# Softmax scaling on VectorE, products held behind a subtraction, and a rearranged start, in a fused softmax-convolution and tanh MLP

## The chip, the cores and the metric

The kernel runs on one core of a Trainium2 chip. A time is device microseconds of one execution. The kernel before takes 772.08 us (median of 3 runs, 771.82 to 773.02, so within 0.16% of each other). The span of a profile is some 2 us shorter than the time of the run it belongs to (769.8 against 771.89 us for the kernel before).

## The reference

```python
# x: (8, 4096, 192)   weight_gen: (8, 4096, 8 heads, 7)   w_in: (192, 2048)   w_out: (2048, 192)
w = softmax(weight_gen, axis=-1)
x_pad = six rows of zeros in front of each sequence of x
a[b, s, h, g] = sum over k < 7 of w[b, s, h, k] * x_pad[b, s + k, h, g]      # h: head, g: 24 channels
h   = a.reshape(32768, 192) @ w_in
out = (h - tanh(h)) @ w_out
```

## The kernel before

The 32,768 tokens go in 32 superblocks of 1024. For superblock n, ScalarE takes exp of the weights; VectorE sums over k and takes the reciprocal; GpSimd scales the exponentials by it and makes the seven products (tap k of x times its weight), six of them in pairs; a DMA of GpSimd's queue adds the three odd products onto the even ones (the **accumulating DMA**). TensorE adds up and transposes the products by multiplying them with an identity (**conv**, tile pc), ScalarE copies the result out of PSUM (convT), TensorE makes 16 tiles of the hidden layer (**gemm1**, "f tiles", tile ph), ScalarE takes tanh, VectorE subtracts, and TensorE makes the **second product** (gemm2) of the superblock before, between the f tiles. The order of every engine's instructions is fixed by hand.

```python
    def softmax_norm(n):                                   # VectorE
        e_t = e_of.pop(n)
        nc.vector.reduce_sum(out=zsum[:], in_=..., axis=AX.X)
        zr = wgpool.tile([P, J * H], FP32, name="zr")      # in SBUF
        nc.vector.reciprocal(zr[:], zsum[:])
        zr_of[n] = (e_t, zr)
    ...
    def products(n, on_vector=(), hooks={}):
        ...
        scale(nc.gpsimd, wsm[:], e_t, zr)                  # GpSimd
        ...                                                # seven products, accumulating DMA
    ...
    def conv(n, chunks): ...       # matmuls into one bank pc, then ONE copy to convT
    ...
    for n in range(NTOT):
        if n + 3 < NTOT:
            load(n + 3)
        if n + 2 < NTOT:
            products(n + 2)        # as soon as GpSimd gets there
        for p in range(J):
            gemm1(n, 2 * p)
            gemm1(n, 2 * p + 1)
            if p == 5 and n + 3 < NTOT:
                softmax_exp(n + 3)
            if n >= 1:
                gemm2((n - 1) * J + p)
            if n + 1 < NTOT:
                if p == (6 if n > 0 else 7):
                    conv(n + 1, (0, 1))
                    conv(n + 1, (2,))
            if p == 6 and n + 3 < NTOT:
                softmax_norm(n + 3)
```

gemm1 and conv share three PSUM buffers (tag "ph"), so an f tile may start only when the subtraction of the tile three places back has read its buffer (in the trace one such subtraction ends at 298.68 us and gemm1 begins at 298.74).

The softmax here doesn't subtract the row's maximum and nothing guards it: scores larger than these inputs give would overflow.

## Time and profile before

| | before |
|---|---|
| time | 772.08 us |
| TensorE busy / GpSimd busy, of a 769.8 us span | 735.1 / 695.0 us |
| superblock 1 begins (first matmul of gemm1 after conv(1)) | 46.92 us |
| conv(3), conv(31) begin | 93.37, 728.13 us |
| steady round, conv to conv | 22.63 us |

Read it so: from conv(3) on, all rounds but one take 22.63 us, with TensorE busy for 22.61 of them; the one longer round holds the 1.16 us stop that the prediction mentions. On this reading a gain must come from the first 93 us, and a loss can come from anywhere. The page and chain rows are in the prediction.

### The profile page before, as it was taken

To read this page: it belongs to the slowest core of one execution; us is meant where nothing else is said; L and a number is where in the kernel's file an instruction comes from. 1 tells how busy PE (TensorE), PEld (TensorE's weight loads), DVE (VectorE), ACT (ScalarE), POOL (GpSimd) and SP (SyncE) were. 2 spreads that over 40 slices of the span, in tenths; PEclk is the share of its full clock that TensorE was granted. 3 is DMA by queue.
4 is the path that set the end of the run, shared out by engine and by line. 5 is a ranking of instruction groups with operands and counts; after the bars stand their busy time and mean duration, and the time that the engine had idled before them with its cause. 6 is when DMAs were issued, how large, how long until landed. Compare 5 with 4: busy or idle time off the path is not lost.

```text
span 769.8 us, 32365 instructions
## 1 busy us (share of the span) xinstructions
PE 735.1 (95%) x14784; PEld 581.3 (76%) x14784; DVE 653.3 (85%) x594; ACT 640.8 (83%) x865; POOL 695.0 (90%) x291
## 2 busy tenths in 40 slices
PE   1688999999999999999999999999999999999997
PEld 1357777877787877877788778787787777787777
DVE  5876988888898888888888889888888988888883
ACT  1677888888888888888888888888888888888883
POOL 5999999999999999999999999999999999999100
PEclk9899999999999999999999999999999999999999
DMA  8813776555677555577655557765556775542412
GB/s 214 183 75 86 182 182 144 125 144 148 169 181 173 133 130 147 151 178 181 168 119 139 145 159 181 181 132 144 138 149 168 181 181 120 127 139 66 98 43 83
DMA packets 25848, 111.37 MB, mean 145 GB/s; under 512 B 4801, under 2 KB 9457, under 8 KB 21625
## 3 DMA queue, kind: packets, MB, share of 16 engines
q1 hardware_dynamic: 14688, 76.95, 29.9%
q0 software_dynamic: 10816, 31.99, 25.9%
q8 instruction: 115, 1.88, 1.0%
q10 hardware_dynamic: 208, 0.39, 0.2%
q14 instruction: 21, 0.16, 0.1%
HBM read 54.49 MB, written 25.17 MB: 103 GB/s over the span
## 4 chain that ended last, share of the span: by engine, by line
PE 93%; DMA 2%; DVE 2%; issue 1%; POOL 1%; ACT 0%; SPq 0%; POOLq 0%; DVEq 0%; ACTq 0%
PE ph L233 43%; PE po L264 43%; PE pc L210 6%; DVE gt L244 2%; PE po L305 1%; DMA x_t<-in_x_dram 1%; DMA w_in<-in_moe_w_in_dram 1%; DMA wg_t<-in_weight_gen_dram 1%; POOL even L167 0%; ACT th L242 0%; DVE zsum L128 0%; DVE zr L132 0%; POOL w_in L340 0%; SPq L99 0%; SPq L348 0%
## 5 line engine op out<-in xcount | busy, mean ns | idle before, releaser
L244 DVE TENSOR_TENSOR gt<-ph,th 128x1024 bf16<-128x1024 f32 x512 | 602.6, 1219 | 91.6 <-ACT th L242 91.4
L242 ACT ACTIVATE th<-ph 128x1024 f32<-128x1024 f32 x512 | 497.1, 1022 | 63.6 <-PE ph L233 63.2
L233 PE MATMUL ph<-convT,w_in 64*128 64x512 bf16 x3072 | 381.3, 378 | 7.7 <-DVE gt L244 6.8
L264 PEld LDWEIGHTS <-gt 64*128 64x128 bf16 x7936 | 344.4, 94 | 52.5 <-ACT th L242 1.7
L264 PE MATMUL po<-w_out,gt 64*128 64x192 bf16 x7936 | 373.8, 243 | 1.7 <-ACT th L242 1.3
L167 POOL TENSOR_TENSOR even<-x_t,wsm 128x1536 bf16<-128x1536 f32 x94 | 272.8, 2903 | 3.9 <-DMA x_t<-in_x_dram 1.5
L167 POOL TENSOR_TENSOR odd<-x_t,wsm 128x1536 bf16<-128x1536 f32 x92 | 267.0, 2903 | 0.0
L233 PEld LDWEIGHTS <-w_in 64*128 64x128 bf16 x3072 | 179.6, 94 | 109.5 <-issue 13.4
L167 POOL TENSOR_TENSOR last<-x_t,wsm 128x1536 bf16<-128x1536 f32 x31 | 103.4, 3335 | 0.0
L289 ACT ACTIVATE out_sb<-po 128x192 f32<-128x192 f32 x248 | 81.9, 330 | 9.1 <-PE po L264 3.2
L220 ACT ACTIVATE convT<-pc 128x1024 bf16<-128x1024 f32 x64 | 48.7, 808 | 33.4 <-PE pc L210 33.4
L210 PE MATMUL pc<-ident,even 64*128 64x64 bf16 x2304 | 47.8, 191 | 18.4 <-POOL even L167 16.8
L210 PEld LDWEIGHTS <-even 64*128 64x128 bf16 x2304 | 42.2, 96 | 19.2 <-POOL even L167 17.0
L136 POOL TENSOR_TENSOR wsm<-e_t,zr 128x448 f32<-128x448 f32 x32 | 44.4, 1387 | 6.0 <-DVE zr L132 6.0
L176 POOL DMA_DIRECT2D even<-odd x29 | 34.9, 1205 | 9.0 <-POOL odd L167 9.0
L118 ACT ACTIVATE e_t<-wg_t 128x448 f32<-128x448 f32 x32 | 18.5, 578 | 10.9 <-DMA wg_t<-in_weight_gen_dram 10.9
L128 DVE TENSOR_REDUCE zsum<-e_t 128x64 f32<-128x448 f32 x32 | 19.5, 609 | 4.8 <-ACT e_t L118 4.8
L210 PE MATMUL pc<-ident,last 64*128 64x64 bf16 x768 | 22.9, 191 | 0.0
L132 DVE RECIPROCAL zr<-zsum 128x64 f32<-128x64 f32 x32 | 17.7, 553 | 3.2
L210 PE MATMUL pc<-ident,odd 64*128 64x64 bf16 x448 | 15.3, 195 | 3.1 <-issue 3.1
L210 PEld LDWEIGHTS <-last 64*128 64x128 bf16 x768 | 16.8, 96 | 0.0
L210 PEld LDWEIGHTS <-odd 64*128 64x128 bf16 x448 | 11.0, 99 | 3.3 <-issue 3.3
(18 smaller groups left out, 48.0 us busy)
## 6 DMA issues: line engine op xcount, KB each, us to landing
x_t<-in_x_dram SPq DMA_DIRECT2D x24, 1344.0 KB
even<-odd POOLq DMA_DIRECT2D x29, 1024.0 KB, 8.8
out_dram<-out_sb SPq DMA_DIRECT2D x31, 768.0 KB
x_t<-in_x_dram SPq DMA_DIRECT2D x8, 1176.0 KB
wg_t<-in_weight_gen_dram SPq DMA_DIRECT2D x32, 224.0 KB
x_t<-in_x_dram SPq DMA_DIRECT2D x8, 157.5 KB
w_in<-in_moe_w_in_dram POOLq DMA_DIRECT2D x6, 128.0 KB, 7.1
w_out<-in_moe_w_out_dram POOLq DMA_DIRECT2D x1, 768.0 KB, 8.0
```

The source lines that it names most:

```text
L118: nc.scalar.activation(out=e_t[:].rearrange("p j h k -> p (j h k)"), in_=wg_t[:].rearrange("p j h k -> p (j h k)"), func=ACT.Exp,)
L128: nc.vector.reduce_sum(out=zsum[:], in_=e_t[:].rearrange("p j h k -> p (j h) k"), axis=AX.X)
L136: eng.tensor_mul(wsm.rearrange("p j h k -> p (j h) k"), e_t[:].rearrange("p j h k -> p (j h) k"), zr[:].rearrange("p (n o) -> p n o", o=1) ...
L167: eng.tensor_mul(dst[k].rearrange("p c j h g -> p j h c g"), x_t[:, k : k + J, :].rearrange("p j (h c g) -> p j h c g", h=H, c=NC), w[:, : ...
L176: nc.gpsimd.dma_start(out=even[:].rearrange("p i c j h g -> p (i c j h g)")[:, 0:ACC], in_=odd[:].rearrange("p i c j h g -> p (i c j h g)" ...
L210: nc.tensor.matmul(pc[:, r, col : col + R], lhsT=prods[c][gi][r * R : (r + 1) * R, c, 2 * j : 2 * j + 2].rearrange("p j h g -> p (j h g)") ...
L220: nc.scalar.activation(out=convT[:, c0 : c0 + nch, :].rearrange("p c (j r t) -> p r (c j) t", r=2, t=R), in_=pc[:, :, 0 : nch * JH * R].re ...
L233: nc.tensor.matmul(ph[:, r, :], lhsT=w_in[r * R : (r + 1) * R, c, f * P : (f + 1) * P], rhs=convT[r * R : (r + 1) * R, c, :], start=(c == ...
L242: last_act[0] = nc.scalar.activation(out=th[:], in_=ph_f, func=ACT.Tanh)
L244: nc.vector.tensor_sub(gt[:], ph_f, th[:])
L264: mm = nc.tensor.matmul(po[:, 0:D], lhsT=g_of[n][f][r * R : (r + 1) * R, col : col + P], rhs=w_out[r * R : (r + 1) * R, f, :], start=(r == ...
L289: last_act[0] = nc.scalar.activation(out=out_sb[:, j, :], in_=po[:, 0:D], func=ACT.Copy)
```

## The change

Its intent: take the softmax scaling off GpSimd (all but that of superblock 2); let GpSimd begin the products of a superblock at a fixed place in the round; and shorten the start. Cut to its core:

```diff
+    obank = [psum_o.tile([P, 512], FP32, name=f"obank{i}", tag=f"obank{i}") for i in range(2)]
...
+    def softmax_norm(n, bank, in_psum=False):
+        e_t, zsum = softmax_sum(n)
+        zr = bank[:, 512 - J * H : 512]          # 1/sum into a PSUM bank: conv's own
+        nc.vector.reciprocal(zr, zsum[:])
...
+        wsm = wgpool.tile([P, J, H, K], FP32, name="wsm")
+        last_wsm[0] = scale(nc.vector, wsm[:], e_t, zr)
...
-        scale(nc.gpsimd, wsm[:], e_t, zr)
...
+            if k == 0 and behind is not None:
+                order(mul, behind, "pace")       # first product waits for a subtraction
...
     for n in range(NTOT):
-        if n + 2 < NTOT:
-            products(n + 2)
         for p in range(J):
             gemm1(n, 2 * p)
             gemm1(n, 2 * p + 1)
...
+            if p == 0 and 1 <= n < NTOT - 2:
+                products(n + 2, behind=last_sub[0] if n > 1 else None)
             if n + 1 < NTOT:
                 if p == (6 if n > 0 else 7):
                     conv(n + 1, (0, 1))
-                    conv(n + 1, (2,))
+                if p == (6 if n > 1 else 7):
+                    bank = conv(n + 1, (2,))
...
-                softmax_norm(n + 3)
+                softmax_norm(n + 3, bank if n > 0 else obank[0])
```

At the start (not shown): the loads of weights and x are split and reordered, the second half of w_in is issued behind GpSimd's third product instead of its first, VectorE makes four instead of five of the first products, and conv(0) works on both of its parts at once.

More of the change, by code (lines that the diff above doesn't have):

```diff
@@ L59 @@
     psum_h = ctx.enter_context(tc.tile_pool(name="psum_h", bufs=3, space=bass.MemoryType.PSUM))
-    psum_o = ctx.enter_context(tc.tile_pool(name="psum_o", bufs=2, space=bass.MemoryType.PSUM))
+    psum_o = ctx.enter_context(tc.tile_pool(name="psum_o", bufs=1, space=bass.MemoryType.PSUM))
     ident = const.tile([P, P], BF16, name="ident")
     make_identity(nc, ident[:])
+    obank = [psum_o.tile([P, 512], FP32, name=f"obank{i}", tag=f"obank{i}") for i in range(2)]
     zero = const.tile([1, D], FP32, name="zero")
@@ L69 @@
     e_of = {}
-    zr_of = {}
+    wsm_of = {}
     prods_of = {}
@@ L74, with order, load_wg @@
     last_act = {}
-    def load(n):
+    g1_act = {}
+    last_sub = {}
+    last_wsm = {}
+    def order(inst, other, reason):
+        tc.add_manual_dep(
+            inst.ins,
+            other.ins.name,
+            mybir.DependencyInfo(mybir.DependencyClass.Sync, mybir.DependencyReason.DATA),
+            reason=reason,
+        )
+    def load_wg(n):
         b, s = divmod(n, NSB)
@@ L83, in load, with load_x @@
         )
+        wg_of[n] = wg_t
+    def load_x(n):
+        b, s = divmod(n, NSB)
+        s0 = s * TOK
         x_t = xpool.tile([P, HALO + J, D], FP32, name="x_t")
@@ L111, in load @@
             rows(0, P)
-        wg_of[n] = wg_t
         x_of[n] = x_t
@@ L123, in softmax_exp, with softmax_sum @@
         e_of[n] = e_t
-    def softmax_norm(n):
+    def softmax_sum(n):
         e_t = e_of.pop(n)
@@ L130, in softmax_norm, with softmax_norm_gpsimd, products @@
         )
+        return e_t, zsum
+    def softmax_norm(n, bank, in_psum=False):
+        e_t, zsum = softmax_sum(n)
+        zr = bank[:, 512 - J * H : 512]
+        nc.vector.reciprocal(zr, zsum[:])
+        wsm_v = None
+        if in_psum:
+            wsm_v = obank[n % 2][:, 0 : J * H * K].rearrange("p (j h k) -> p j h k", j=J, h=H)
+            scale(nc.vector, wsm_v, e_t, zr)
+        wsm = wgpool.tile([P, J, H, K], FP32, name="wsm")
+        last_wsm[0] = scale(nc.vector, wsm[:], e_t, zr)
+        wsm_of[n] = (wsm, wsm_v)
+    def softmax_norm_gpsimd(n):
+        e_t, zsum = softmax_sum(n)
         zr = wgpool.tile([P, J * H], FP32, name="zr")
         nc.vector.reciprocal(zr[:], zsum[:])
-        zr_of[n] = (e_t, zr)
+        wsm = wgpool.tile([P, J, H, K], FP32, name="wsm")
+        scale(nc.gpsimd, wsm[:], e_t, zr[:])
+        wsm_of[n] = (wsm, None)
     def scale(eng, wsm, e_t, zr):
-        eng.tensor_mul(
+        return eng.tensor_mul(
             wsm.rearrange("p j h k -> p (j h) k"),
             e_t[:].rearrange("p j h k -> p (j h) k"),
-            zr[:].rearrange("p (n o) -> p n o", o=1).to_broadcast([P, J * H, K]),
+            zr.rearrange("p (n o) -> p n o", o=1).to_broadcast([P, J * H, K]),
         )
-    def products(n, on_vector=(), hooks={}):
+    def products(n, on_vector=(), sums=None, hooks={}, behind=None):
         x_t = x_of.pop(n)
-        e_t, zr = zr_of.pop(n)
-        wsm_v = None
-        if on_vector:
-            pw = psum_o.tile([P, 512], FP32, name="pw", tag="po")
-            wsm_v = pw[:, 0 : J * H * K].rearrange("p (j h k) -> p j h k", j=J, h=H)
-            scale(nc.vector, wsm_v, e_t, zr)
-        wsm = wgpool.tile([P, J, H, K], FP32, name="wsm")
-        scale(nc.gpsimd, wsm[:], e_t, zr)
+        wsm, wsm_v = wsm_of.pop(n)
         in_pairs = n not in PLAIN
@@ L166, in products @@
             eng, w = (nc.vector, wsm_v) if k in on_vector else (nc.gpsimd, wsm[:])
-            eng.tensor_mul(
+            mul = eng.tensor_mul(
                 dst[k].rearrange("p c j h g -> p j h c g"),
@@ L189, in products, with conv @@
         else:
-            prods_of[n] = [[dst[k] for k in sorted(range(K), key=lambda k: k in on_vector)]] * NC
-    def conv(n, chunks):
+            prods_of[n] = [[dst[k] for k in (sums or range(K))]] * NC
+    def conv(n, *parts):
         prods = prods_of[n]
@@ L197, in conv @@
         convT = conv_of[n]
-        nch = len(chunks)
-        pc = psum_h.tile([P, 2, HT], FP32, name="pc", tag="ph")
-        steps = [
-            (gi, ci, c)
-            for gi in range(max(len(prods[c]) for c in chunks))
-            for ci, c in enumerate(chunks)
-            if gi < len(prods[c])
-        ]
-        for si, (gi, ci, c) in enumerate(steps):
-            for j in range(JH):
-                col = (ci * JH + j) * R
-                for r in range(2):
-                    nc.tensor.matmul(
-                        pc[:, r, col : col + R],
-                        lhsT=prods[c][gi][r * R : (r + 1) * R, c, 2 * j : 2 * j + 2].rearrange(
-                            "p j h g -> p (j h g)"
-                        ),
-                        rhs=ident[r * R : (r + 1) * R, r * R : (r + 1) * R],
-                        start=(si == 0 and j == 0),
-                        stop=(si == len(steps) - 1 and j == JH - 1),
-                    )
@@ L219, in conv @@
-        c0 = chunks[0]
-        nc.scalar.activation(
-            out=convT[:, c0 : c0 + nch, :].rearrange("p c (j r t) -> p r (c j) t", r=2, t=R),
-            in_=pc[:, :, 0 : nch * JH * R].rearrange("p r (cj t) -> p r cj t", t=R),
-            func=ACT.Copy,
-        )
-        if c0 + nch == NC:
+        pcs = [psum_h.tile([P, 2, HT], FP32, name="pc", tag="ph") for _ in parts]
+        for gi in range(max(len(g) for g in prods)):
+            for chunks, pc in zip(parts, pcs):
+                some = [c for c in chunks if gi < len(prods[c])]
+                last = gi == max(len(prods[c]) for c in chunks) - 1
+                for c in some:
+                    for j in range(JH):
+                        col = ((c - chunks[0]) * JH + j) * R
+                        for r in range(2):
+                            nc.tensor.matmul(
+                                pc[:, r, col : col + R],
+                                lhsT=prods[c][gi][
+                                    r * R : (r + 1) * R, c, 2 * j : 2 * j + 2
+                                ].rearrange("p j h g -> p (j h g)"),
+                                rhs=ident[r * R : (r + 1) * R, r * R : (r + 1) * R],
+                                start=(gi == 0 and c == chunks[0] and j == 0),
+                                stop=(last and c == some[-1] and j == JH - 1),
+                            )
@@ L226, in conv @@
+        for chunks, pc in zip(parts, pcs):
+            c0, nch = chunks[0], len(chunks)
+            nc.scalar.activation(
+                out=convT[:, c0 : c0 + nch, :].rearrange("p c (j r t) -> p r (c j) t", r=2, t=R),
+                in_=pc[:, :, 0 : nch * JH * R].rearrange("p r (cj t) -> p r cj t", t=R),
+                func=ACT.Copy,
+            )
+        if parts[-1][-1] == NC - 1:
             prods_of.pop(n)
+        return pcs[-1][:, 0]
     def gemm1(n, f):
@@ L241, in gemm1 @@
         ph_f = ph[:].rearrange("p r t -> p (r t)")
+        g1_act[0] = last_act.get(0)
         last_act[0] = nc.scalar.activation(out=th[:], in_=ph_f, func=ACT.Tanh)
         gt = gpool.tile([P, TOK], BF16, name=f"gt{f}", tag=f"gt{f}")
-        nc.vector.tensor_sub(gt[:], ph_f, th[:])
+        last_sub[0] = nc.vector.tensor_sub(gt[:], ph_f, th[:])
         g_of.setdefault(n, []).append(gt)
@@ L258, in gemm2 @@
             if r == 0:
-                half[blk] = psum_o.tile([P, 512], FP32, name="po")
+                half[blk] = obank[blk % 2]
             ops.append((r, n, j, half[blk]))
@@ L271, in gemm2 @@
                 if r == 1 and f == 0 and i in (1, LAST):
-                    tc.add_manual_dep(
-                        mm.ins,
-                        last_act[0].ins.name,
-                        mybir.DependencyInfo(
-                            mybir.DependencyClass.Sync, mybir.DependencyReason.DATA
-                        ),
-                        reason="order of the row tiles in a bank",
-                    )
+                    order(mm, g1_act[0] if i == 1 else last_act[0], "row tiles in one bank")
         if i > 0:
@@ L332, in load_w_out, with load_w_in, copy_w_in, rest_of_w_in @@
         nc.gpsimd.dma_start(out=w_out[:], in_=moe_w_out.rearrange("(c p) e -> p c e", c=NFT))
-    HF = F // 2
-    def load_w_in(q):
+    FA = 8 * P
+    def load_w_in(f0, f1):
         for c in range(NC):
-            src = moe_w_in[c * GC : c * GC + 1, q * HF : (q + 1) * HF]
-            nc.gpsimd.dma_start(
-                out=w_in[0:R, c, q * HF : (q + 1) * HF],
+            src = moe_w_in[c * GC : c * GC + 1, f0:f1]
+            dma = nc.gpsimd.dma_start(
+                out=w_in[0:R, c, f0:f1],
                 in_=bass.AP(
-                    tensor=src.tensor, offset=src.offset, ap=[[G * F, H], [F, GC], [1, HF]]
+                    tensor=src.tensor, offset=src.offset, ap=[[G * F, H], [F, GC], [1, f1 - f0]]
                 ),
             )
-    def copy_w_in(q, eng):
-        eng.dma_start(
-            out=w_in[R:P, :, q * HF : (q + 1) * HF], in_=w_in[0:R, :, q * HF : (q + 1) * HF]
-        )
-    load(0)
+            if f0 == 0:
+                order(dma, last_wsm[0], "order of the loads")
+    def copy_w_in(f0, f1, eng):
+        eng.dma_start(out=w_in[R:P, :, f0:f1], in_=w_in[0:R, :, f0:f1])
+    def rest_of_w_in():
+        load_w_in(FA, F)
+    load_wg(0)
+    load_x(0)
     softmax_exp(0)
-    softmax_norm(0)
-    load(1)
+    softmax_norm(0, obank[0], in_psum=True)
+    load_wg(1)
+    load_x(1)
+    load_w_in(0, FA)
     products(
         0,
-        on_vector=(1, 3, 4, 5, 6),
-        hooks={-1: lambda: load_w_in(0), 0: lambda: load_w_in(1)},
+        on_vector=(3, 4, 5, 6),
+        sums=(3, 0, 4, 5, 1, 6, 2),
+        hooks={2: rest_of_w_in},
     )
     softmax_exp(1)
-    softmax_norm(1)
-    copy_w_in(0, nc.scalar)
-    copy_w_in(1, nc.sync)
+    softmax_norm(1, obank[1], in_psum=True)
+    load_wg(2)
+    copy_w_in(0, FA, nc.scalar)
+    copy_w_in(FA, F, nc.sync)
     products(1, on_vector=(0, 1), hooks={4: load_w_out})
-    conv(0, (0, 1))
-    conv(0, (2,))
-    load(2)
-    softmax_exp(2)
-    softmax_norm(2)
+    conv(0, (0, 1), (2,))
+    load_x(2)
     for n in range(NTOT):
         if n + 3 < NTOT:
-            load(n + 3)
-        if n + 2 < NTOT:
-            products(n + 2)
+            load_wg(n + 3)
+            load_x(n + 3)
         for p in range(J):
@@ L378 @@
             gemm1(n, 2 * p + 1)
+            if n == 0 and p == 1:
+                softmax_exp(2)
             if p == 5 and n + 3 < NTOT:
@@ L385 @@
                     conv(n + 1, (0, 1))
-                    conv(n + 1, (2,))
-            if p == 6 and n + 3 < NTOT:
-                softmax_norm(n + 3)
+                if p == (6 if n > 1 else 7):
+                    bank = conv(n + 1, (2,))
+            if n == 0 and p == 2:
+                softmax_norm_gpsimd(2)
+                products(2)
+            if p == (7 if n == 1 else 6) and n + 3 < NTOT:
+                softmax_norm(n + 3, bank if n > 0 else obank[0])
     gemm2(LAST)
```

## The prediction

Its sum came to +0.7 us, 772.8 in all. The passages marked as cut, here and in three of the expectations, are statements on the hardware that did not come from this case's traces, or that rest on such. That the stops of conv(2) are late fetches was my reading at that time, and that splitting conv(2) would shrink them to about half (gain 1.5 of the measured 2.78 us) a guess.

> **What bounds the kernel now.** I read the page's busy shares first, then the chain of waits that ended last, then that chain over one superblock, then the order of time on VectorE and ScalarE at the one place where they come close to TensorE. From the page:
>
> ```profile
> PE 735.1 (95%) x14784; PEld 581.3 (76%) x14784; DVE 653.3 (85%) x594; ACT 640.8 (83%) x865; POOL 695.0 (90%) x291
> PE 93%; DMA 2%; DVE 2%; issue 1%; POOL 1%; ACT 0%; SPq 0%; POOLq 0%; DVEq 0%; ACTq 0%
> ```
>
> From the chain in order of time, one superblock (start us, length us, what):
>
> ```profile
> 297.21 1.52 PE pc L210 x104
> 298.72 0.02 issue
> 298.74 1.47 PE ph L233 x12
> 300.21 1.32 PE po L264 x32
> 301.53 1.30 PE ph L233 x12
> ```
>
> TensorE is 93% of the chain. From 93.54 us on, a superblock takes 22.63 us in the windows view, with TensorE busy 22.61 of it at a granted clock of 1.00. GpSimd looks almost as full (22.25 of 22.63), but no wait of TensorE on a product stands in that part of the chain: conv starts when the stream reaches it. The parts that are not TensorE's lie in the first 75 us; these rows of the chain show them:
>
> ```profile
> 19.98 4.79 DMA wg_t<-in_weight_gen_dram
> ...
> 26.20 0.55 DVE zr L132
> 26.75 1.09 DVE gt L244
> ...
> 51.42 1.03 ACT th L242
> 52.44 0.05 issue
> 52.49 1.49 PE po L264 x31
> ...
> 67.20 0.82 issue
> 68.02 2.04 PE pc L210 x128
> 70.07 1.96 issue
> 72.03 0.59 PE pc L210 x29
> ```
>
> The reader is to see four delays: the third block of weights (wg_t) arrives late and holds VectorE's first subtraction to 26.67; superblock 0 then runs at VectorE's pitch until TensorE begins superblock 1 at 46.92; the second product's first matmul waits for a tanh (52.49); conv(2) stops twice with nothing to wait for (0.82 + 1.96).
>
> [...] Here six pairs of row tiles take 1.29 to 1.30 us, 0.216 each[...]. [...] The trace's GpSimd scaling takes 0.97 us at 36.48 and 57.55 but 1.33 at 5.20 beside VectorE's own two-input scaling[...]. [...] The new code puts 1/sum into conv's own bank, so it must wait for the copy of that bank; no run here shows it yet. [...] Between the two stops of conv(2) lie exactly 128 matmuls with their 128 weight loads, so I read both stops as late fetches; splitting conv(2) over two places should soften them.
>
> **The change, part by part.**
>
> *GpSimd's scaling goes.* 29 instructions of about 1.42 us leave GpSimd in the steady part (row L136, 1387 ns mean over 32). GpSimd's round falls from 22.64 us (scalings start at 283.57 and 306.20) to about 21.2. Worth on the path: 0, since TensorE never waited for it there.
>
> *Pacing.* Products of a superblock now wait for an early subtraction; in the compiled order it is the second (f tile 1) of superblock n, not a later one. It ends at 305.6 on the old clock. Six products at a pitch of 2.86 us end at 322.8; the accumulating DMA lands 8.8 us (its row) after its issue near 323.1, so at 332; conv needs it at 342.5. Slack 10 us, cost 0. Early on GpSimd lags: products(2) should end near 57, products(3) near 77.5 with its DMA at 83, against conv(3) near 85. Tight, but no wait.
>
> *Start, gains.* At 9.85 both engines have x. VectorE has four products instead of five: it ends near 16.6, then sum 0.61, reciprocal 0.55, two scalings of 0.63 to 19.05, two products of 1.75 to 22.4. GpSimd's third product ends at 9.89 + 3 x 2.86 = 18.5; the last 24 conv matmuls and two copies (1.02, 0.59) put the first gemm1 at 20.3 and its tanh's end at 22.3. So the first subtraction starts at about 22.4 instead of 26.67: 4.2 us. Given back: the sum and reciprocal of block 2 move inside the subtractions (1.25), and block 3's scaling adds 0.65. 14 subtractions took 16.8 us before (26.67 to 43.47); 22.4 + 16.8 + 1.25 + 1.95 + 2.3 for the last two gives 44.6, against 46.9: gain 2.3 to 3, I take **2.5**. It needs the second half of w_in, issued only after 18.5, in both halves of SBUF before f tile 8 at about 29.5: old issues took 7 us to land and the copy about 4, so it is due at 28 to 29.5.
> The second product's wait moves one tanh earlier: **0.9** (52.44 to 51.52). The two fetch stops, 2.78, should shrink to about half: **1.5**. The split makes gemm1 of superblock 2 wait for the copy of the third chunk: give back **0.3**.
>
> *Steady part, loss.* The order of time of VectorE, then of ScalarE, over one conv (start, length):
>
> ```profile
> 298.61 0.61 DVE L128 TENSOR_REDUCE zsum<-e_t 128x64 f32<-128x448 f32 x1
> 299.32 0.55 DVE L132 RECIPROCAL zr<-zsum 128x64 f32<-128x64 f32 x1
> 300.66 2.35 DVE L244 TENSOR_TENSOR gt<-ph,th 128x1024 bf16<-128x1024 f32 x2 [0.79 <-ACT th L242]
> ```
>
> ```profile
> 298.18 1.51 ACT L220 ACTIVATE convT<-pc 128x1024 bf16<-128x1024 f32 x2 [0.60 <-PE pc L210]
> 299.60 1.94 ACT L242 ACTIVATE th<-ph 128x1024 f32<-128x1024 f32 x2
> ```
>
> VectorE has 0.79 us to spare before the subtraction of f tile 14, and the added scaling (0.63) would just fit. But the reciprocal must now wait for the second conv copy, which ends at 299.69, instead of starting at 299.32. Then: reciprocal 299.72 to 300.27; scaling, after a gap of 0.10 like that between sum and reciprocal here, 300.38 to 301.01; subtraction 14 starts at 300.93 (consecutive VectorE instructions overlap by about 0.08) instead of 300.66 and ends at 302.14. Its buffer is the one that gemm1's f tile 1 of the next superblock writes: three buffers, 16 + 2 tiles a superblock, so the place repeats each time. That tile starts at 301.35 + 0.65 = 302.00 today. TensorE follows the end of a subtraction by about 0.055 (the subtraction before this conv ends at 298.68, a row at 296.33 of length 2.35, and gemm1 begins at 298.74), so it would start at 302.20: **0.2 us lost** in each of 27 superblocks (2 to 28), 5.3 us. Everything after it has slack again, and the round becomes about 22.83 us.
>
> Sum: -2.5 - 0.9 - 1.5 + 0.3 + 5.3 = +0.7 us.
>
> **The rivals.** (a) *The steady wait isn't there.* Subtraction 14 need only end 0.14 us sooner than I work out for no wait at all; a shorter gap between reciprocal and scaling (0.03 as between other instructions) gives half of it. For: such tuned code was probably laid so as to fit. Against: the wait for the copy is in the compiled program. Then only the start counts: about 767. (b) *GpSimd was the hidden bound*, its round of 22.64 being TensorE's: then its freed 1.4 us a round would bring up to 40 us. Against: when TensorE stopped for 1.16 us at 343.94, the next conv still found its products ready, and gemm1 and the second product alone fill the round at full clock. I give it almost nothing. (c) *A transfer at the start comes too late*, the second half of w_in above all, or the accumulating DMA for conv(3): 1 to 4 us of the gain is lost, and the time is 774 to 777. (d) *VectorE becomes the bound*: 19.92 + 0.63 of 22.63 leaves room; only the local wait above is real.
>
> **Range and chances.** The sum gives 772.8. The loss has more room to shrink than to grow (it sits on margins of 0.1 us), so I predict 771. Rival (a) with a better start gives 765; (c) on top of the sum, or a wait of 0.35 us, gives 777. To be 2% faster the kernel would have to lose 15.4 us, more than all delays of the start that this change touches (4.2 + 0.9 + 2.8); to be 2% slower the round would have to grow by 0.75 us with a gain of 5 at the start. Chances: faster 0.03, same 0.94, slower 0.03.
>
> **What would show it.** Right: a round of about 22.8 between convs, with a wait of TensorE on the subtraction before f tile 1 of each superblock; GpSimd near 21 us a round with idle time that ends at a subtraction; superblock 1 beginning near 44.6; no wait of VectorE on wg_t. Wrong in size: a round still 22.63 (then the time is near 767), or over 23. Wrong in kind: TensorE waiting on products or on the accumulating DMA at conv, VectorE's scaling taking 1 us or more, GpSimd's products longer than 2.90, or a wait on w_in at f tile 8.

## The result, and the profile after

The changed kernel takes **772.24 us** (median of 4 runs, 772.03 to 773.02); the kernel before took 772.51 in the same rounds. The ratio is 0.9999, 95% interval 0.9982 to 1.0016. The result is the same time, out of two large opposite terms:

| | before | after |
|---|---|---|
| superblock 1 begins | 46.92 | 44.30 |
| conv(3) begins | 93.37 | 88.33 |
| steady round | 22.63 | 22.82 |
| conv(31) begins | 728.13 | 728.02 |
| span of the profile | 769.8 | 770.0 |

The lead of 5.0 us at conv(3) is down to 0.1 us at conv(31). From the changed kernel's page, busy times and the chain:

```profile
PE 740.4 (96%) x14784; PEld 578.0 (75%) x14784; DVE 668.6 (87%) x624; ACT 640.9 (83%) x865; POOL 668.3 (87%) x261
PE 93%; DVE 3%; POOL 1%; DMA 1%; ACT 1%; issue 1%; SPq 0%; POOLq 0%; DVEq 0%
```

GpSimd (POOL) lost 27 us of work and VectorE (DVE) gained 15, yet the shares of the chain are nearly those of before: busy time moved, the path did not. The start, in the chain of waits (start us, length us, what):

```profile
41.97 2.28 DVE gt L277 x2
44.25 0.04 issue
44.30 1.58 PE ph L265 x12
...
47.87 1.03 ACT th L275
48.91 0.05 issue
48.95 1.49 PE obank L297 x31
...
67.03 0.94 issue
...
69.72 0.61 ACT convT L251
```

Superblock 1 begins 2.62 us sooner. The second product's wait (48.95) lies 4.65 us behind that, instead of 5.57: another 0.92. Near conv(2) one stop with no cause is left (67.03, 0.94), and the split of conv(2) has made a new wait on a copy (69.72). One conv of the steady part, first the chain, then VectorE's order of time (the bracket gives the idle time ahead of an instruction and what ended it):

```profile
299.00 0.65 PE ph L265 x6
299.65 0.02 issue
299.67 0.82 PE ph L265 x6
```

```profile
296.08 0.61 DVE L145 TENSOR_REDUCE zsum<-e_t 128x64 f32<-128x448 f32 x1
297.19 0.56 DVE L154 RECIPROCAL pc<-zsum 128x64 f32<-128x64 f32 x1 [0.51 <-ACT convT L251]
297.86 0.62 DVE L172 TENSOR_TENSOR wsm<-e_t,pc 128x448 f32<-128x448 f32 x1
298.40 4.70 DVE L277 TENSOR_TENSOR gt<-ph,th 128x1024 bf16<-128x1024 f32 x4
```

Before, two f tiles stood here in one piece of 12 matmuls and 1.30 us; now they are two pieces of six, 1.49 us together: the first matmul of the second piece comes 0.39 us behind the one ahead of it, where the other pairs (two row tiles) come 0.20 behind theirs. VectorE's rows show the reason: the reciprocal stands idle for 0.51 us until ScalarE's copy of conv's bank is done, then reciprocal, scaling and subtraction follow one another. GpSimd's waits hold one new row, the pacing (us in total, times, longest):

```profile
POOL even L195 <- DVE gt L277: 28.2, 25, 1.4
```

### The profile page after: what moved, and what is told of

Read it like the earlier page. It is cut to its first block, busy times and chain, and to the rows that moved or that the text cites. A ratio compares the mean times of both kernels' runs of the same rounds, so it can differ in the third digit from the quotient of the medians.

```text
span 770.0 us, 32309 instructions
## 1 busy us (share of the span) xinstructions
PE 740.4 (96%) x14784; PEld 578.0 (75%) x14784; DVE 668.6 (87%) x624; ACT 640.9 (83%) x865; POOL 668.3 (87%) x261
## 4 chain that ended last, share of the span: by engine, by line
PE 93%; DVE 3%; POOL 1%; DMA 1%; ACT 1%; issue 1%; SPq 0%; POOLq 0%; DVEq 0%
PE ph L265 43%; PE obank L297 43%; PE pc L240 6%; DVE gt L277 2%; PE po L331 1%; DMA x_t<-in_x_dram 1%; POOL even L195 1%; ACT convT L251 0%; ACT th L275 0%; POOL odd L195 0%; DVE wsm L172 0%; DVE zsum L145 0%; SPq L117 0%; DVE pc L154 0%; DVE obank L154 0%
## 5 line engine op out<-in xcount | busy, mean ns | idle before, releaser
L265 PE MATMUL ph<-convT,w_in 64*128 64x512 bf16 x3072 | 385.5, 377 | 7.5 <-DVE gt L277 5.3
L297 PE MATMUL obank<-w_out,gt 64*128 64x192 bf16 x7936 | 373.9, 243 | 1.8 <-issue 0.9
L195 POOL TENSOR_TENSOR even<-x_t,wsm 128x1536 bf16<-128x1536 f32 x94 | 276.8, 2945 | 29.3 <-DVE gt L277 28.2
L195 POOL TENSOR_TENSOR odd<-x_t,wsm 128x1536 bf16<-128x1536 f32 x93 | 273.8, 2945 | 0.0
L265 PEld LDWEIGHTS <-w_in 64*128 64x128 bf16 x3072 | 175.8, 94 | 117.2 <-issue 20.4
L315 ACT ACTIVATE out_sb<-obank 128x192 f32<-128x192 f32 x248 | 82.2, 331 | 14.1 <-PE obank L297 8.7
L154 DVE RECIPROCAL pc<-zsum 128x64 f32<-128x64 f32 x28 | 15.7, 561 | 14.8 <-ACT convT L251 14.8
L172 DVE TENSOR_TENSOR wsm<-e_t,pc 128x448 f32<-128x448 f32 x28 | 17.4, 622 | 2.9
```

Of the source, the lines that this page charges most:

```text
L172: return eng.tensor_mul(wsm.rearrange("p j h k -> p (j h) k"), e_t[:].rearrange("p j h k -> p (j h) k"), zr.rearrange("p (n o) -> p n o", ...
L195: mul = eng.tensor_mul(dst[k].rearrange("p c j h g -> p j h c g"), x_t[:, k : k + J, :].rearrange("p j (h c g) -> p j h c g", h=H, c=NC), ...
L265: nc.tensor.matmul(ph[:, r, :], lhsT=w_in[r * R : (r + 1) * R, c, f * P : (f + 1) * P], rhs=convT[r * R : (r + 1) * R, c, :], start=(c == ...
L297: mm = nc.tensor.matmul(po[:, 0:D], lhsT=g_of[n][f][r * R : (r + 1) * R, col : col + P], rhs=w_out[r * R : (r + 1) * R, f, :], start=(r == ...
L315: last_act[0] = nc.scalar.activation(out=out_sb[:, j, :], in_=po[:, 0:D], func=ACT.Copy)
```

## The experiments

Two things were to be settled. First: is the 0.19 us a round really the wait for the copy, worked out in the prediction? Second: the prediction said of the pacing that it costs nothing and of GpSimd's relief that it is worth nothing, so pacing should be of no account. All runs gave correct results.

| run | time, median | before, same rounds | ratio, 95% interval |
|---|---|---|---|
| scaling back on GpSimd | 770.84 | 771.36 | 0.9994 [0.9982, 1.0005] |
| no pacing | 779.65 | 771.36 | 1.0119 [1.0091, 1.0148] |
| 1/sum in SBUF | 771.21 | 771.36 | 0.9998 [0.9986, 1.0011] |
| before + VectorE scaling | 786.25 | 771.36 | 1.0190 [1.0150, 1.0230] |
| before + VectorE scaling + pacing | 774.01 | 772.05 | 1.0029 [1.0016, 1.0042] |
| f tile 1 later | 767.80 | 772.05 | 0.9944 [0.9931, 0.9956] |
| f tiles 1, 14, 15 later | 764.30 | 772.05 | 0.9904 [0.9890, 0.9918] |
| 1/sum in the bank, then in SBUF | 768.41 | 772.05 | 0.9956 [0.9942, 0.9969] |
| pacing behind f tile 5 | 788.14 | 771.11 | 1.0221 [1.0207, 1.0235] |
| pacing behind f tile 7 | 809.62 | 771.11 | 1.0500 [1.0486, 1.0515] |
| useless work ahead of the reciprocal | 772.13 | 771.11 | 1.0015 [1.0003, 1.0028] |
| useless work behind the scaling | 778.54 | 770.89 | 1.0099 [1.0082, 1.0116] |

### The steady loss

**Scaling back on GpSimd** (pacing and start as changed):

```diff
-                softmax_norm(n + 3, bank if n > 0 else obank[0])
+                softmax_norm_gpsimd(n + 3)
```

> The changed kernel with the steady scaling back on GpSimd (1/sum in SBUF), its start, order and pacing kept. Theory (start gains about 5.2 us, the VectorE chain conv copy, reciprocal, scaling, subtraction 14 gives 0.19 us back in each of 27 rounds): round from conv to conv back to 22.63 us, no wait of TensorE on the subtraction before f tile 1, time 767.1 (766.4 to 768). Rival A (the start's gain is not kept, and the scaling costs nothing): time stays at 772.2. Rival B (the later, paced begin of the products costs the time): stays at 772.2 with the round at 22.82, or gets worse since GpSimd's round is 22.6 again.

Measured: 770.84 us. The undisturbed rounds are back at 22.63 and the gap before f tile 1 is gone, so the scaling's place on VectorE did cause it. But the time is a miss by nearly 4 us: seven stops of TensorE that wait for nothing the profile shows, from 68 to 256 us, took the rest (5.8 us together, where the changed kernel has three with 1.8). They led to the second question, below.

**Useless work on VectorE, ahead of the reciprocal and behind the scaling**: a reduction of 0.32 us, in superblocks 4 to 31.

```diff
         e_t, zsum = softmax_sum(n)
+        if n > 3: nc.vector.reduce_sum(out=zd[:, 0:24], ...)     # first run: here
         zr = bank[:, 512 - J * H : 512]
         nc.vector.reciprocal(zr, zsum[:])
         ...
         last_wsm[0] = scale(nc.vector, wsm[:], e_t, zr)
+        if n > 3: nc.vector.reduce_sum(out=zd[:, 0:24], ...)     # second run: here
```

> The changed kernel with a useless reduction of 24 x 7 elements (about 0.32 us on VectorE) between the sum and the reciprocal, in superblocks 4 to 31. Theory (the reciprocal waits for conv's copy, which ends about 0.4 us behind the sum, so VectorE has idle time just there): costs 0, 772.2 and a round of 22.82, though VectorE gets 28 x 0.32 = 9 us more work. Rival (VectorE is short of time round conv, whatever it does): the round grows by 0.3 us to 23.1 and the time to 780.

> The changed kernel with the same useless reduction (about 0.32 us on VectorE), now behind the scaling instead of ahead of the reciprocal. Theory (from the end of conv's copy on, VectorE's reciprocal, scaling and subtraction 14 set when gemm1 of f tile 1 may start, with no slack left): each of 27 superblocks loses another 0.32 us, round 23.14, time 772.2 + 8.6 = 780.8, range 778.5 to 783. Rival (the wait before f tile 1 is set by something else, or there is slack): 772 to 774, as with the reduction ahead of the reciprocal.

Measured: 772.13 us with the round still 22.82, and 778.54 us with a round of 23.06. The same 9 us of VectorE work costs nothing in one place and 6.3 us (778.54 less the changed kernel's 772.24) two instructions later. (The two stood on different chips; by the ratios the first costs up to about 1 us and the second 7.7, so I go by the rounds, which repeat to 0.01.) The chain of the second run shows the whole loop in order:

```profile
298.93 0.60 ACT convT L258
...
299.55 0.57 DVE pc L154
...
300.21 0.62 DVE wsm L179
300.84 0.24 DVE zd L164
301.07 1.14 DVE gt L284
302.22 0.04 issue
302.26 0.82 PE ph L272 x6
```

Copy, reciprocal, scaling, extra work, subtraction 14, f tile 1. The extra instruction shows as 0.24 and not as its 0.32, since consecutive VectorE instructions overlap by 0.08; 27 x 0.24 = 6.5 us is what was measured. The expectation had used the instruction's length, not its step on the chain.

**1/sum in SBUF**, so that the scaling need not wait for the copy; both of its inputs are then in SBUF:

```diff
-                softmax_norm(n + 3, bank if n > 0 else obank[0])
+                softmax_norm(n + 3, None)          # None: zr is a tile in SBUF
```

> The changed kernel with 1/sum in SBUF, scaling still on VectorE: no wait for conv's copy, but two SBUF inputs while GpSimd runs products of 2.90 us. Theory 1 [...]: VectorE's scaling starts only when the running product ends, up to 2.9 us late, mean near 1.4, so TensorE loses about 1 us or more a round: 795 to 815. Theory 2 [...]: reciprocal at the end of the sum, 0.4 us sooner, subtraction 14 starts when its tanh ends, round 22.63 and time near 767.

Measured: 771.21 us, a steady round of 22.63, and three early scalings that took 1.67, 3.02 and 2.52 us. Behind the first, superblock 1 begins 1.8 us later than in the changed kernel (46.09); behind the other two TensorE stands for 2.1 and 1.4 us. VectorE's and GpSimd's orders of time around the worst of them:

```profile
72.59 3.02 DVE L175 TENSOR_TENSOR wsm<-e_t,zr 128x448 f32<-128x448 f32 x1
```

```profile
72.23 2.90 POOL L198 TENSOR_TENSOR odd<-x_t,wsm 128x1536 bf16<-128x1536 f32 x1
```

GpSimd's product ends at 75.13 and the scaling, which takes 0.62 us with 1/sum in the bank, at 75.61, 0.48 behind it. That the product held it is my reading of these times. In the steady part the end of a product (300.45) and the issue of the accumulating DMA (300.75) come just there, the scaling takes about 0.85 us (300.08 to 300.93), and it costs nothing: the round is 22.63. **1/sum in the bank for superblocks 3 to 6, then in SBUF** joins the two:

```diff
+                softmax_norm(n + 3, obank[0] if n == 0 else bank if n < 4 else None)
```

> The changed kernel with 1/sum in the bank only while GpSimd still lags (superblocks 3 to 6), then in SBUF, where the scaling need not wait for conv's copy. Theory (with pacing the scaling falls between two products of GpSimd[...]; in the run with 1/sum in SBUF from the start it cost up to 2.5 us three times early on): round 22.63 from superblock 5 on and time 772.2 - 24 x 0.195 = 767.5, range 766.5 to 769. Rival ([...] later scalings are held too): 770 to 773.

Measured: 768.41 us. The first SBUF scaling still took 1.40 us, the later ones take from 0.62 to about 0.86; from conv(6) on every round is 22.63.

**f tile 1 later**: gemm1 of f tile 1 goes into the second product that follows it, so that TensorE has other work until subtraction 14 is done; **f tiles 1, 14 and 15 later** does the same for the two behind conv.

```diff
+            if n > 1 and p == 0:
+                gemm1(n, 0)
+                inside[3] = lambda n=n: gemm1(n, 1)           # second run: inside[6], and
+            elif 1 < n < NTOT - 1 and p == J - 1:             # these three lines
+                inside[2] = lambda n=n: (gemm1(n, 2*J - 2), gemm1(n, 2*J - 1))
             else: ...
-                gemm2((n - 1) * J + p)
+                gemm2((n - 1) * J + p, inside)                # calls inside[f] behind step f
```

> The changed kernel with gemm1 of f tile 1 moved into the second product that follows it (behind its f = 3) for superblocks 2 to 31, so that TensorE has other work until subtraction 14 has ended. Theory (the steady loss is that one wait and nothing else): the round goes from 22.82 back to 22.63 and the time to 772.2 - 27 x 0.195 = 767.0, range 766 to 769. Rival (something else comes due as the round shortens, as where the scaling went back to GpSimd and fetch stops took the gain): 770 to 773.

> As the run before it, and also gemm1 of f tiles 14 and 15 inside the second product that follows them (behind its f = 2), so that the matmuls behind conv do not wait for conv's copies. Estimate: round 22.58, time 765.5; rival (nothing more to gain there[...]): 767, the same as the run before it; if the later subtractions of f tiles 14 and 15 make a new wait, 769 or more.

Measured: 767.80 us with a round of 22.63, and 764.30 us with a round of 22.50. In its rounds the first takes the prediction's steady loss back whole; the time fell by 4.4 us and not by 5.1, as one fetch stop near 113 us was longer (1.39 us between two starts, 0.79 in the changed kernel). The second goes below the round of the kernel before: the 12 matmuls behind conv, 1.47 us there, take their bare 1.29 when six matmuls (three pairs) of the second product stand between conv's end and them:

```profile
293.38 1.52 PE pc L240 x104
294.90 0.25 PE obank L297 x6
295.15 1.29 PE ph L265 x12
```

This version beats the kernel before by about 1% (interval 0.9890 to 0.9918), and with it the changed kernel, which takes the same time.

### What the pacing does

**No pacing** (one word of the changed kernel undone), and **before + VectorE scaling** (start as before, no pacing, scaling from conv's bank for superblocks 4 to 31):

```diff
-                products(n + 2, behind=last_sub[0] if n > 1 else None)
+                products(n + 2, behind=None)
```

> The changed kernel with the products of a superblock no longer ordered behind a subtraction. Theory: pacing is worth 0, time 772.2 within 0.6 and the round 22.82; GpSimd's idle time only moves to another wait. Rival B (pacing costs or saves TensorE something, by the time at which the accumulating DMA and the loads run): differs by more than 1 us, and the round is not 22.82.

> The kernel before with only the steady scaling of superblocks 4 to 31 moved to VectorE, 1/sum in conv's PSUM bank; start, order and no pacing as before. Theory: round 22.82 to 22.83 instead of 22.63 from superblock 1 or 2 on, 28 rounds, so 772.5 + 5.3 = 777.8 (777 to 778.5). Rival A (the steady part is neutral): 772.5. If GpSimd had been the hidden bound: faster than before.

Measured: 779.65 and 786.25 us, 7 and 8 us over what was expected. Undisturbed rounds are 22.82 in both, as they should be; the rest is stops of TensorE of 0.3 to 2 us with no cause in the profile ("issue"). (The second run's times spread from 780.57 to 791.71 us, and its profile is of the slowest, so its stops are at the high end.) To find the cause I looked at the trace for what the stops have in common:

- Counting TensorE's matmuls, weight loads and the 35 recorded instructions of its sequencer in order of start, from 0, the first instruction behind such a stop is number 193 past a multiple of 256. In the traces of all 14 kernels there are 95 places, from 60 to 735 us, where a gap between starts at this position of the 256 exceeds 0.42 us; every other gap of that size has a wait that the chain names, or sits among matmuls slowed behind one.
- Each of the 95 ends 2.2 to 2.9 us (median 2.4) behind the start of a packet on the instruction queue, which the page lists with 115 packets of 16 KB: one for every 256 of TensorE's 29,603 recorded instructions.

So I read these stops as late fetches of the next 256 instructions (a "block" from here on: the recorded instructions from one such position to the next). What differed between kernels was where the data transfers lay. The prediction's rule for pacing asked only whether products and their DMA are in time; in the two kernels without pacing they are, but a freed GpSimd works up to the release of its buffers, and its accumulating DMA and the loads of x behind it then run from the start of conv on. The share of the 16 DMA engines' time taken by data, in the first 4 us of a conv (conv(4) to conv(28)), against the stops:

| kernel | DMA share, first 4 us of conv | fetch stops over 0.42 us, sum of gaps less 0.2 each |
|---|---|---|
| before | 0.00 | 3, 3.9 us |
| changed | 0.00 | 3, 1.8 us |
| scaling back on GpSimd | 0.02 (0.14 in the first 2 us of conv(4) to (10)) | 7, 5.8 us |
| no pacing | 0.79 | 12, 7.0 us |
| before + VectorE scaling | 0.87 | 16, 16.0 us |
| before + VectorE scaling + pacing | 0.00 | 2, 1.0 us |
| pacing behind f tile 5 | 0.16 (0.84 in the 2 us ahead of conv) | 19, 17.6 us |
| pacing behind f tile 7 | 0.53 (0.86 in the 2 us ahead) | 22, 34.7 us |

The six other kernels, all paced, have a share of 0.01 or less and one or two stops each. A table like this is no proof: the last three rows were made to test it.

**Before + VectorE scaling + pacing**: the run that took 786 us, with the products ordered behind the subtraction of f tile 1.

```diff
+            if p == 0 and 1 <= n < NTOT - 2:
+                products(n + 2, behind=last_sub[0] if n > 1 else None)
```

> The kernel before with its start unchanged, the softmax scaling of superblocks 4 to 31 on VectorE from conv's bank (as in the run that took 786.3), and now also the products ordered behind the second subtraction. Theory (pacing pins the DMA traffic away from TensorE's instruction fetch): the fetch stops go, the 0.195 us a superblock of the wait before f tile 1 stays: 772.1 + 27 x 0.195 = 777.4, range 775.5 to 779. Rival 1 (the scaling on VectorE or the bank itself made the stops, pacing has nothing to do with it): still 784 to 788. Rival 2 (it is the changed start, not the pacing, that kept the changed kernel free of stops): over 782.

Measured: 774.01 us, 12 us less than without pacing. From conv(5) on every round is 22.82 with no other stop. It is 3.4 us below what was expected: conv(3) begins 2.0 us sooner than in the kernel before, as the stops at conv(2) are shorter, and the stop of 1.16 us that the kernel before has in one later round is gone too. The rival that only the changed start keeps the stops away is out.

**Pacing behind f tile 5, behind f tile 7** (from superblock 4 on): the transfers move later by 5 and 8 us, with nothing else changed.

```diff
-            if p == 0 and 1 <= n < NTOT - 2:
+            if p == (2 if n > 3 else 0) and 1 <= n < NTOT - 2:      # 3 in the second run
```

> The changed kernel with its pacing moved later by two pairs of f tiles from superblock 4 on: the products are ordered behind the subtraction of f tile 5 instead of f tile 1, some 5.2 us later in the round. Six products and their accumulating DMA then end at about 337 on the old clock, 5 us before conv needs them, so no wait on them is due. In the changed kernel the transfers of a round run from about 4 us behind the start of conv to 4 us before the next one; moved by 5.2 us their tail lies on the next conv. Theory (where the transfers lie against conv is what counts, since conv takes instructions fastest): fetch stops come back in part, 773 to 777. Rival (it is enough that GpSimd is held back at all, or the stops without pacing had another cause): 772.2, round 22.82 with no stops.

> The same one pair later, behind the subtraction of f tile 7, some 7.8 us later than in the changed kernel: transfers from about 12 us behind conv to 4 us behind the next one, so that they cover conv; the accumulating DMA is due 2.8 us before conv needs it. Theory (place of the transfers): stops as in the kernel without pacing, 777 to 782, without a wait of TensorE on the accumulating DMA. Rival (any pacing does): 772.2. A third way: the DMA is late and conv waits for it, which the chain would show as a wait on that DMA and not as a stop without a cause.

Measured: 788.14 and 809.62 us, far over what the theory asked for and in its direction; the rival that any pacing will do is out. Neither has a wait of TensorE on the accumulating DMA; the waits of TensorE list conv's stops as "issue" (us in total, times, longest), in the run with f tile 5:

```profile
PE pc L240 <- issue: 16.4, 15, 2.2
```

The windows view shows one conv of the changed kernel, then one of the run with f tile 7 (window, its length, busy time and count of PE, PEld, DVE, ACT, POOL, then granted clock, DMA share, GB/s):

```profile
317.32:319.32 2.00, 1.98 (x113) 1.76 (x110) 2.00 (x3) 1.37 (x3) 2.00 (x2) 1.00 0.03 8
```

```profile
180.80:182.20 1.40, 1.40 (x100) 1.40 (x97) 1.40 (x2) 0.77 (x3) 1.40 (x1) 1.00 0.81 298
182.20:185.90 3.70, 0.24 (x16) 0.11 (x7) 0.84 (x2) 0.83 (x1) 3.70 (x2) 1.00 0.61 242
```

In the changed kernel the DMA engines are all but idle (0.03) while conv runs 113 matmuls in 2 us. In the other, conv begins under a share of 0.81, and TensorE then stands for 3.5 us at full clock, with no wait that the profile shows, at a block's end.

Why conv of all places: 104 matmuls and their 104 weight loads take 1.52 us there, so at that rate a block would last 256 / 208 x 1.52 = 1.9 us (an estimate), less than the 2.2 us or more measured between the start of a late block's packet and its first instruction. (The blocks round a steady conv hold other matmuls too; those with at least 100 of conv's instructions last 3.9 us in the median of the changed kernel.) At the rate of gemm1 (12 matmuls and 12 loads in 1.29 us) a block would last 13.8 us, at that of the second product (32 and 32 in 1.32 us) 5.3 us. The counts fit this: 90 of the 95 stops come right behind a block that holds instructions of conv, and of 714 blocks that hold none only 5 were followed by a stop. A superblock has 14784 x 2 / 32 = 924 such instructions and one recorded semaphore instruction, 157 over three blocks, so a boundary falls near a conv in only some rounds; the run with f tile 5 stops in about every second one.

The packets show where a late block loses its time. I took the 1,472 block boundaries from 60 to 735 us of the 14 traces, the n-th packet as that of the n-th boundary. A block's packet begins a little behind the first instruction of the block before it: 0.5 us in the median where data took at most 0.02 of the DMA engines round that instruction (from 2 us ahead of it to 1 us behind it), and 3.7 us where data took over 0.95. The packet itself lasts 1.05 us in the first case and 0.96 in the second. So the packet of a late block begins late; it is not slower once it runs. This also fits that the run with f tile 7, with less DMA in the first 4 us of conv (0.53) than the one without pacing (0.79), loses five times as much (34.7 us against 7.0). By these medians it is the traffic at the moment when the block before begins that goes with a late packet; for a block full of conv this moment lies mostly ahead of conv, where the run with f tile 7 has a share of 0.86 and the one without pacing 0.10. Behind blocks with at least 100 of conv's instructions, the next packet began 0.3 us (median) after the block's first instruction in the changed kernel and in the one without pacing, 1.2 us with f tile 5 and 2.7 us with f tile 7. What holds the packet back was not shown.

## Why the prediction was right, and where it was not

The time, 772.24 us, lies in the range of 765 to 777, and the two large terms were of the right kind and size.

- **Start, 2.5 predicted**: 2.62 (44.30 against 46.92). The first subtraction began at 22.94 instead of the predicted 22.4. VectorE no longer waits for a late block of weights.
- **Second product, 0.9**: 0.92.
- **Fetch stops of conv(2), 1.5**: 1.84 (0.82 + 1.96 fell to 0.94).
- **Copy wait of the split, 0.3 given back**: 0.65. Together with the line above, 1.19 against 1.2. The sum of these terms, 4.7, is the lead of 5.0 us at conv(3) but for 0.3 that I did not trace.
- **Steady loss, 0.195 us a round**: 22.82 less 22.63 is 0.19, times 27 is 5.1 us. The two runs with useless work show that the loop runs through the copy, reciprocal, scaling and subtraction 14; the run with f tile 1 later takes the loss back. The gap between reciprocal and scaling was 0.11 (predicted 0.10), so rival (a), no steady wait, fell. The lean from 772.8 to 771 in its favour was not borne out: the sum was nearer. It rested on a margin of 0.14 us where the prediction's own figures give 302.20 - 302.00 = 0.20.
- **GpSimd was the hidden bound (b)**: fell. Its busy time fell by 27 us and no round got shorter. The relief was mis-sized: 0.9 us a round (22.25 busy of 22.63 before, 21.35 of 22.82 now) and not 1.42, since the scaling's record overlapped that of the product ahead of it by 0.5 (280.71 + 3.36 = 284.07, scaling from 283.57).
- **No gain expected in the steady rounds** (TensorE busy for 22.61 of 22.63 us): not quite. With the same 14,784 matmuls, f tiles 1, 14 and 15 later has a round of 22.50 instead of 22.63.
- **A late transfer (c)**: not seen; TensorE's longest wait on w_in cost about 1 us within a stretch set by VectorE. **VectorE as the bound (d)**: fell; 9 us more of its work cost nothing when put ahead of the wait.
- **The step that failed is "cost 0" of the pacing, with "Worth on the path: 0" of GpSimd's relief.** Both asked only whether TensorE waits for a product. Without pacing the changed kernel takes 7.4 us more (779.65 less 772.24; 9 by the ratios), and the relief added to the kernel before it costs 12 us more than with pacing. The pacing cost nothing, but it was worth all of that, and the total came out right because the relief's cost and the pacing's worth cancel. In this part the right total was luck. I had read the two stops at conv(2) as late fetches, and had not asked what else might bring fetches late in the later convs. In the kernel before, GpSimd's round of 22.64 us matched TensorE's, and the transfers stayed off conv (share 0.00) with no pacing; that the equal rounds are the reason was not tested.

## What to carry to other kernels

A freed engine is not free: ask what it will now start earlier, and what that start (here the transfers) will lie on top of (without pacing 779.65 us, with it 772.24). Look whether stops that have no wait in the profile recur at one position: here they came at number 193 past a multiple of 256, which I read as late instruction fetches, and what helped was to keep data transfers away from the stretch with the densest instructions and from the few us ahead of it (786.25 to 774.01 us). Work on an engine with idle time cost by its place here, not by its length (the same 9 us nothing in one place, 6.3 us in the other): find the wait in front of which it is free. When two terms of a sum cancel, undo them one at a time before believing either.
